# Turning the keys inside the scores' matmuls, and the last output product in quarters

## The chip, the cores and the metric

The kernel runs on one core of a Trainium2 chip. The metric is device time in microseconds. Three runs of the kernel before took 295.28, 295.98 and 296.2 us; the median is 295.98. The engines are TensorE (PE in the profile; PEld is its loading of stationary operands), VectorE (DVE), ScalarE (ACT), GpSimd (POOL) and SyncE (SP, which here only issues transfers).

## The reference

Two stages follow each other. The first is a gated linear attention, a recurrence over 768 positions for 4 batches of 8 heads of 48 dimensions:

```python
for t in range(S):
    state = alpha[:, :, t, :, None] * state + np.einsum('bhd,bhe->bhde', k[:, :, t], v[:, :, t])
    y[:, :, t] = np.einsum('bhd,bhde->bhe', q[:, :, t], state)
```

The heads' outputs side by side are x, 384 wide. The second stage is a gated state-space layer: `proj = x @ w_in` (384 by 1024) gives a value and a gate half of 512; `h = a * h + val` runs along the positions; the result is `(silu(gate) * h) @ w_out` (512 by 384).

## The kernel before, in words

Of the two versions in the file, `general` is a fallback that a test of the inputs selects; only `fast` runs here. It cuts the 4 x 768 positions into N = 12 groups m of 256, three to a batch, and each group into two chunks c of 128.

**Attention by chunks.** VectorE makes running products of alpha with a scan (`prod`, L664) and the inverse products with a second (`inv`, L685). Queries are multiplied by the products, keys by their inverses (Z, L694). With that scaling the recurrence becomes an ordinary masked matrix product within a chunk plus a state carried between chunks. Z has position along the free axis and head dimension along partitions. The eight heads form four pairs p, with the two heads i of a pair on partitions 0 to 47 and 64 to 111. The steps for one chunk are these.

- `keys` (L707, L708): for the state, the scaled keys must have position on partitions. Four TensorE transposes (one per pair, against the identity matrix) write them to a PSUM bank, and ScalarE copies that bank to `ktm`. The last chunk of a batch needs no state, so it has no such step: 20 of 24 chunks have it.
- `scores` (L717): eight products of 48 rows, keys stationary and queries moving, 128 by 128 each. The two heads of a pair go to two different banks. Each fp32 product is two instructions.
- `masks`: the near head's scores are multiplied by a triangular mask on VectorE straight from PSUM (L734); the far head's are copied by ScalarE (L729) and masked by GpSimd (L730).
- `state` (L766, L769), `values` (L745), `carried` (L756): the chunk's update of the state, the product of masked scores with v, and the contribution of the state before the chunk. The last two add up in PSUM tiles `ys`.
- `join` copies ys to SBUF and moves rows by transfer into `xT`, the input of the second stage.

**Second stage.** `block(n, cc)` makes one quarter cc of the 512 inner columns: twelve instructions of 256 columns on TensorE (L801: six for the value, six for the gate), the scan `hh` on VectorE (L809), Silu on ScalarE (L816), and their product f on GpSimd (L817). `output(n)` multiplies f by w_out: sixteen instructions of 384 columns (L831), of which the last quarter's come last. ScalarE copies the two results of 128 by 384 out (L839), in the last pass VectorE does (L841), and SP stores them (L842).

**Order.** The order of the program is written by hand; the engines run their own instructions in that order and meet through semaphores. The first groups are handled separately before the loop. Pass n of the loop then handles, interleaved, the second stage of group n, the attention of group m = n + 1, and on VectorE the products of group n + 2. Those products are a generator, `products(n + 2)`, whose steps `go` puts between the other work: first the transpose of alpha (L650) and small steps, then the prod scan, then the inv scan, then the transpose of k, its product with the inverses, the transpose of q and its product. In pass 1, group m = 2 comes from inputs in natural layout, so the passes' bodies differ.

In a pass n > 1 TensorE's order is: keys of both chunks, scores of both chunks, blocks 0 and 1, state/values/state/carried, blocks 2 and 3, output. In pass n = 1 it is: blocks 0 and 1, keys, scores, block 2, state/values/carried, block 3, output. `products`' first step stands ahead of the masks, so VectorE transposes alpha while the scores run.

**PSUM.** There are eight banks: one for the state `st`; b0, b1 and b6, through which `mm` rotates for blocks, key transposes and outputs; and the four banks b23 (a pair of banks in one tile), b4 and b5, which `pair_of` gives out in turn to scores and to ys.

Of the kernel before, what the change touches and what calls it, by code (L numbers as in the profile page):

```python
# [10 lines left out]
FP32 = mybir.dt.float32  # L11
# [335 lines left out]
def fast(  # L347
# [33 lines left out]
    def pool(name, bufs, **kw):  # L381
        return ctx.enter_context(tc.tile_pool(name=name, bufs=bufs, **kw))
# [1 line left out]
    const = pool("const", 1)  # L384
    p1 = pool("p1", 1)
    p2 = pool("p2", 2)
    p3 = pool("p3", 3)
    p4 = pool("p4", 4)


    ps_st = pool("ps_st", 1, space=PS)
    ps = pool("ps", 1, space=PS)
    next_mm, next_pair = itertools.cycle("016"), itertools.cycle((0, 1))

    def mm(*dims, b=None):
        return ps.tile([C, *dims], FP32, tag=f"b{b or next(next_mm)}", name="mm")

    def pair_of(*dims, dtype=FP32):
        if next(next_pair):
            return [ps.tile([C, *dims], dtype, tag=f"b{b}", name="pair") for b in (4, 5)]  # L400
        t = both()
        n = dims[0] * dims[1]
        return [t[:, i, 0:n].rearrange("p (x y) -> p x y", x=dims[0]).bitcast(dtype) for i in range(2)]

    def both():
        return ps.tile([C, 2, 4 * C], FP32, tag="b23", name="pair")


    NR = 2
# [60 lines left out]
    mask = const.tile([C, C], FP32, name="mask")  # L470
    a_log = const.tile([NI, C], FP32, name="a_log")
    a_dec = const.tile([C, NI], FP32, name="a_dec")
    ktms = [const.tile([C, 4, 2, 64], FP32, name=f"ktm{i}") for i in range(2)]


    aT = const.tile([C, 4 * GC + 1], FP32, name="aT")
# [20 lines left out]
    def constants():  # L497
        nc.vector.memset(first, FLOOR)
        make_identity(nc, ident)
        for name in "akq":  # L500
            nc.vector.memset(natural(name, 0)[:, :, :, D:64], 1.0)

        nc.gpsimd.memset(mask, 1.0)
        nc.gpsimd.affine_select(out=mask, in_=mask, compare_op=ALU.is_ge, fill=0.0, base=0,
                                channel_multiplier=-1, pattern=[[1, C]])
        for t in vs:
            nc.gpsimd.memset(t[:, :, :, D:64], 0.0)
        for name in "akq":
            nc.gpsimd.memset(natural(name, 1)[:, :, :, D:64], 1.0)
        for t, x in ((minus, -1.0), (start_p, FIRST_PRODUCT), (last, 0.0), (aT[:, 4 * GC:], 0.0), (one, 1.0)):  # L510
            nc.vector.memset(t, x)
        for m in range(2):
            for name in "akq":
                nc.gpsimd.memset(raw_bufs[m][name].rearrange("p h n -> p (h n)")[:, G * H * 64:], 1.0)
# [72 lines left out]
        nc.vector.tensor_copy(out=flag, in_=fl)  # L587


    Zs = {}  # L590

    def turned(name, m, c, tp):

# [2 lines left out]

    def natural_qk(m, name, c, tp):

        if m not in Zs:
            Zs[m] = p2.tile([C, 4, 2, GC], FP32, tag="Z", name="Z")  # L600
        turned(name, m, c, tp)

        def times():
            i, by = {"k": (1, invs), "q": (0, prods)}[name]
            cols = ds(c * C, C)
            if m < 1:
                by = (inv_c[c][:, 1:] if name == "k" else prod_c[c]).rearrange("p (h n) -> p h n", h=4)
            else:
                by = by[:, :, cols]
            nc.vector.tensor_mul(Zs[m][:, :, i, cols], tp, by)  # L610
        return times

    def check_alpha(m):
# [32 lines left out]
    def products(m, al=None):  # L646
# [40 lines left out]
        yield  # L687
        if m < NAT:
            return
        Z = Zs[m] = p2.tile([C, 4, 2, GC], FP32, tag="Z", name="Z")  # L690
        for name, i, by in (("k", 1, invs), ("q", 0, prods)):
            turn(name, Z[:, :, i])
            yield
            nc.vector.tensor_mul(Z[:, :, i], Z[:, :, i], by)  # L694
            yield


# [3 lines left out]
    def keys(m, c, b=None):  # L701

        if (m % NG) * G + c == NG * G - 1:
            return
        tp = mm(4, C, b=b)
        for p in range(4):
            nc.tensor.transpose(tp[:, p, :], Zs[m][:, p, 1, ds(c * C, C)], ident)  # L707
        nc.scalar.activation(ktms[c].rearrange("p a i d -> p a (i d)"), tp, AF.Copy)  # L708

    def scores(m, c):  # L710
        Z = Zs[m]
        cols = ds(c * C, C)
        sc = pair_of(4, C)
        for p in range(4):
            for i in range(2):
                rows = ds(64 * i, D)
                nc.tensor.matmul(sc[i][:, p, :], Z[rows, p, 1, cols], Z[rows, p, 0, cols], start=True, stop=True)  # L717
        As[m, c] = p2.tile([C, 2, 4, C], FP32, tag="A", name="A"), sc

    def masks(m, c):  # L720
        masks_far(m, c)
        masks_near(m, c)

    def mask_all():
        return mask[:, None, :].to_broadcast([C, 4, C])

    def masks_far(m, c):
        A, sc = As[m, c]
        nc.scalar.activation(A[:, 1], sc[1], AF.Copy)  # L729
        nc.gpsimd.tensor_mul(A[:, 1], A[:, 1], mask_all())  # L730

    def masks_near(m, c):
        A, sc = As[m, c]
        nc.vector.tensor_mul(A[:, 0], sc[0], mask_all())  # L734

    def values(m, c):
        v_sb = vs[m % NV]
        A, _ = As.pop((m, c))
        if c == 0:
            ys[m] = pair_of(2, GC) if m else [mm(2, GC, b=b) for b in "06"]  # L740
        for i in range(2):
            for e in range(2):
                for s in range(2):
                    p = 2 * s + e
                    nc.tensor.matmul(ys[m][i][ds(64 * s, 64), e, ds(c * C, C)], v_sb[:, c, 2 * p + i, :],  # L745
                                     A[:, i, p, :], start=(c == 0 and e == 0), stop=False, skip_group_check=True)

    def carried(m, c):
        ch = (m % NG) * G + c
        if not ch:  # L750
            return
        for e in range(2):
            for s in range(2):
                for i in range(2):
                    p, rows = 2 * s + e, ds(64 * i, D)
                    nc.tensor.matmul(ys[m][i][ds(64 * s, D), e, ds(c * C, C)], S_sbs[ch - 1][rows, p, :],  # L756
                                     Zs[m][rows, p, 0, ds(c * C, C)], start=False, stop=True,
                                     skip_group_check=True)

    def state(m, c):  # L760
        ch = (m % NG) * G + c
        if ch == NG * G - 1:
            return
        for p in range(4):
            for i in range(2):
                nc.tensor.matmul(st[ds(64 * i, 64), p, :], ktms[c][:, p, i, :], vs[m % NV][:, c, 2 * p + i, 0:D],  # L766
                                 start=(ch == 0 and p == 0), stop=(ch == NG * G - 2), skip_group_check=True)
        S_sbs[ch] = p2.tile([C, 4, D], FP32, tag="S_sb", name="S_sb")
        nc.scalar.activation(S_sbs[ch], st, AF.Copy)  # L769
# [53 lines left out]

    def output(n):
        b, g = divmod(n, NG)
        os = [mm(DM) for c in range(G)]

        def part(ccs):
            for c in range(G):
                for cc in ccs:  # L830
                    nc.tensor.matmul(os[c], fs[n][:, cc, ds(c * C, C)], w_out[:, cc, :],  # L831
                                     start=(cc == 0), stop=(cc == NI - 1))

        def finish():
            part(range(split, NI))
            for c in range(G):
                o_sb = p3.tile([C, DM], FP32, tag="o_sb", name="o_sb")
                if n < N - 1:
                    nc.scalar.activation(o_sb, os[c], AF.Copy)  # L839
                else:  # L840
                    nc.vector.tensor_copy(out=o_sb, in_=os[c])  # L841
                nc.sync.dma_start(out=out[b, ds(g * GC + c * C, C), :], in_=o_sb)  # L842

        split = NI - 1 if n else NI // 2
        part(range(split))
        return finish


# [66 lines left out]
    next(steps)  # L915
    masks_near(0, 1)

    k10, q10 = (ps.tile([C, 4, C], FP32, tag=f"b{b}", name="pair") for b in (4, 5))
    natural_qk(1, "q", 0, q10)
    q_sb = p1.tile([C, 4, C], FP32, tag="q_sb", name="q_sb")  # L920
    nc.scalar.activation(q_sb, q10, AF.Copy)
    nc.gpsimd.tensor_mul(Zs[1][:, :, 0, 0:C], q_sb, prods[:, :, 0:C])
    check_alpha(1)
    values(0, 1)
    state(0, 1)
# [61 lines left out]
    for n in range(1, N):  # L987
# [25 lines left out]
            loads(n + 3)  # L1013
        if n + 2 < N:
            load_v(n + 2, SP)
        if att:
            for c in range(G):
                keys(m, c)
            for c in range(G):
                scores(m, c)  # L1020
        go(1)
        if att:
            for c in range(G):
                masks(m, c)
        if n > 1:
            block(n, 0)
            if n == N - 1:
                next(end, None)
            go(1)
            block(n, 1)  # L1030
            go(1)
            attend()
            go(2)
            block(n, 2)
        else:
            block(n, 2)
            go(1)
            attend()
            go(1)
        go(1)  # L1040
        block(n, 3)
        go(10)
# [48 lines left out]
```

## Time and profile before

| | before |
|---|---|
| median of three runs | 295.98 us |
| the profiled execution | 295.81 us |
| its span | 294.1 us |
| TensorE busy | 280.9 us, 96% of the span |
| VectorE busy | 224.9 us, 76% |
| GpSimd busy | 113.7 us, 39% |
| ScalarE busy | 99.5 us, 34% |

The profile is of one execution. Its span is from the first to the last recorded instruction; 1.7 us of its time lie around that. A row of the groups gives the line, engine, operation, tile written and tiles read, shape and count, then busy time and mean duration in ns. Matmuls are pipelined and overlap, so their durations add to more than the time they take, and the distance from one start to the next says more. In the timeline, a row is a run of equal instructions: start in us, length in us, engine, line, operation, tile, shape and count. A last bracket tells how long the engine stood idle before the row and what it waited for.

### The profile page before, as it was taken

What the parts mean: (1) busy time and instruction counts of PE and PEld (TensorE: products, weight loads), DVE (VectorE), ACT (ScalarE), POOL (GpSimd) and SP (SyncE); (2) the same over time, 40 slices, a digit from 0 to 9 for tenths busy, and PEclk for the clock granted to TensorE, in tenths of its full rate; (3) what the DMA queues carried; (4) which work ended last, traced back from release to release, by engine and by line L of the source; (5) the groups of instructions that cost most, each with busy time, mean ns of one, the idle gap of its engine ahead of it and who ended that gap; (6) DMA issues with size and microseconds to landing.
All of it is one profiled execution on the core that took longest, in us unless ns stands there. A gap on an engine that the chain in (4) does not pass through costs nothing.

```text
span 294.1 us, 6126 instructions
## 1 busy us (share of the span) xinstructions
PE 280.9 (96%) x2345; PEld 226.1 (77%) x2345; DVE 224.9 (76%) x269; ACT 99.5 (34%) x220; POOL 113.7 (39%) x116
## 2 busy tenths in 40 slices
PE   7679999999999999999999999999999999999991
PEld 6468877886886896886886896886886886886870
DVE  5898896999996799798699699699699695312311
ACT  2447634433432432432432431431431531331110
POOL 7136792275612612642613513542513523401110
PEclk9999999999999999999999999999999999999999
DMA  9999979999991991991991792991891401101101
GB/s 130 163 175 285 356 128 168 234 271 217 264 177 54 237 167 33 244 187 39 246 171 31 199 213 48 228 196 33 226 204 29 111 10 33 54 15 28 54 7 61
DMA packets 71231, 42.09 MB, mean 143 GB/s; under 512 B 47492, under 2 KB 70536, under 8 KB 71192
## 3 DMA queue, kind: packets, MB, share of 16 engines
q1 hardware_dynamic: 69760, 40.96, 68.5%
q0 software_dynamic: 384, 0.44, 0.7%
q8 instruction: 20, 0.33, 0.5%
q10 hardware_dynamic: 1048, 0.20, 0.4%
q14 instruction: 19, 0.16, 0.2%
HBM read 33.33 MB, written 4.72 MB: 129 GB/s over the span
## 4 chain that ended last, share of the span: by engine, by line
PE 91%; DVE 6%; ACT 1%; issue 0%; DVEq 0%; ACTq 0%
PE mm L801 44%; PE mm L831 21%; PE pair L717 8%; PE pair L745 7%; PE pair L756 3%; PE st L766 3%; PE mm L707 2%; PE st L880 1%; DVE Z L610 1%; PE pair L595 1%; DVE inv L642 1%; DVE prod L664 1%; DVE inv L681 1%; DVE A L734 0%; DVE prod L632 0%
## 5 line engine op out<-in xcount | busy, mean ns | idle before, releaser
L801 PE MATMUL mm<-xT,w_in 128*128 128x256 f32 x576 | 131.1, 384 | 0.0
L801 PEld LDWEIGHTS mm<-xT,w_in 128*128 128x128 f32 x576 | 107.3, 190 | 18.1 <-issue 2.0
L817 POOL TENSOR_TENSOR f<-sg,hh 128x256 f32<-128x256 f32 x48 | 59.0, 1230 | 96.3 <-DVE hh L809 48.6
L831 PE MATMUL mm<-w_out,f 128*128 128x384 f32 x192 | 64.4, 487 | 0.0
L730 POOL TENSOR_TENSOR A<-A,mask 128x512 f32<-128x512 f32 x24 | 30.0, 1271 | 66.6 <-ACT A L729 66.6
L831 PEld LDWEIGHTS mm<-w_out,f 128*128 128x128 f32 x192 | 36.2, 190 | 23.1 <-POOL w_out L555 0.6
L816 ACT ACTIVATE sg<-mm 128x256 f32<-128x256 f32 x48 | 18.4, 384 | 93.9 <-PE mm L801 91.8
L809 DVE TENSOR_TENSOR_SCAN hh<-a_dec,hh,mm 128x256 f32<-128x256 f32 x32 | 23.2, 726 | 20.2 <-PE mm L801 20.1
L734 DVE TENSOR_TENSOR A<-pair,mask 128x512 f32<-128x512 f32 x24 | 16.1, 688 | 27.5 <-ACT A L729 17.7
L664 DVE TENSOR_TENSOR_SCAN prod<-aT,first 128x1024 f32<-128x1024 f32 x10 | 28.1, 2811 | 0.1
L717 PE MATMUL pair<-Z 48*128 48x128 f32 x384 | 25.1, 279 | 1.2 <-DVE first L660 0.9
L685 DVE TENSOR_TENSOR_SCAN inv<-aT,last 128x1025 f32<-128x1025 f32 x10 | 26.0, 2596 | 0.3
L717 PEld LDWEIGHTS pair<-Z 48*128 48x128 f32 x384 | 22.6, 187 | 3.5 <-issue 2.1
L839 ACT ACTIVATE o_sb<-mm 128x384 f32<-128x384 f32 x22 | 10.8, 491 | 42.8 <-PE mm L831 42.8
L745 PE MATMUL pair<-A,v 128*64 128x128 f32 x352 | 21.3, 274 | 0.0
L745 PEld LDWEIGHTS pair<-A,v 128*64 128x64 f32 x352 | 19.1, 137 | 0.0
L650 DVE STREAM_TRANSPOSE aT<-raw_a 128x1024 f32<-128x1024 f32 x9 | 18.4, 2041 | 0.0
L650 DVE STREAM_TRANSPOSE Z<-raw_q 128x1024 f32<-128x1024 f32 x9 | 18.2, 2020 | 0.0
L650 DVE STREAM_TRANSPOSE Z<-raw_k 128x1024 f32<-128x1024 f32 x9 | 18.1, 2015 | 0.0
L729 ACT ACTIVATE A<-pair 128x512 f32<-128x512 f32 x24 | 13.3, 598 | 7.0 <-PE pair L717 5.7
L766 PEld LDWEIGHTS st<-v,ktm 128*64 128x64 f32 x320 | 11.4, 137 | 3.9 <-issue 3.0
L769 ACT ACTIVATE S_sb<-st 128x192 f32<-128x192 f32 x20 | 6.6, 331 | 19.8 <-PE st L766 11.1
(119 smaller groups left out, 255.3 us busy)
## 6 DMA issues: line engine op xcount, KB each, us to landing
raw_k<-in_k_dram SPq DMA_DIRECT2D x24, 192.0 KB, 5.4
raw_q<-in_q_dram SPq DMA_DIRECT2D x24, 192.0 KB, 6.2
v<-in_v_dram SPq DMA_DIRECT2D x24, 192.0 KB, 6.4
out_dram<-o_sb SPq DMA_DIRECT2D x24, 192.0 KB, 1.9
raw_a<-in_alpha_dram SPq DMA_DIRECT2D x23, 192.0 KB, 4.0
raw_a<-in_alpha_dram SPq DMA_DIRECT2D x18, 176.0 KB, 4.2
raw_k<-in_k_dram SPq DMA_DIRECT2D x18, 176.0 KB, 5.7
raw_q<-in_q_dram SPq DMA_DIRECT2D x18, 176.0 KB, 6.6
```

The source lines that it names most:

```text
L650: nc.vector.transpose(out=to.rearrange("p h (c j) -> p h j c", j=NT), in_=raw_bufs[m % NR][name].rearrange("p h (j d) -> p h j d", d=D)[:, ...
L664: nc.vector.tensor_tensor_scan(out=prod, data0=al, data1=first.rearrange("p h n -> p (h n)"), initial=0.0, op0=ALU.mult, op1=ALU.max)
L685: nc.vector.tensor_tensor_scan(out=inv[:, ::-1], data0=aT[:, ::-1], data1=lasts[:, 0:4 * GC + 1][:, ::-1], initial=0.0, op0=ALU.mult, op1= ...
L717: nc.tensor.matmul(sc[i][:, p, :], Z[rows, p, 1, cols], Z[rows, p, 0, cols], start=True, stop=True)
L730: nc.gpsimd.tensor_mul(A[:, 1], A[:, 1], mask_all())
L745: nc.tensor.matmul(ys[m][i][ds(64 * s, 64), e, ds(c * C, C)], v_sb[:, c, 2 * p + i, :], A[:, i, p, :], start=(c == 0 and e == 0), stop=Fal ...
L766: nc.tensor.matmul(st[ds(64 * i, 64), p, :], ktms[c][:, p, i, :], vs[m % NV][:, c, 2 * p + i, 0:D], start=(ch == 0 and p == 0), stop=(ch = ...
L801: nc.tensor.matmul(pj, w_in[cc][:, kk, vg, :], xT[:, kk, :], start=(kk == 0), stop=(kk == NK - 1))
L809: nc.vector.tensor_tensor_scan(out=hh, data0=a_dec[:, cc:cc + 1].to_broadcast([C, GC]), data1=pv, initial=prev_h[cc][:, GC - 1:GC] if n % ...
L816: nc.scalar.activation(sg, pg, AF.Silu)
L817: return lambda: nc.gpsimd.tensor_mul(fs[n][:, cc, :], sg, hhs.pop((n, cc)))
L831: nc.tensor.matmul(os[c], fs[n][:, cc, ds(c * C, C)], w_out[:, cc, :], start=(cc == 0), stop=(cc == NI - 1))
```

## The change

Four things change.

- The transposes of the keys in groups m = 2 to 11 are gone as instructions. The tile of the scaled queries gets 48 more columns on each side that hold an identity matrix on the rows of each head. GpSimd writes them once at the start with eight copies. The scores' product of a chunk that needs turned keys runs over 176 columns, 128 of queries and 48 of identity; so the 48 extra output columns are that head's keys with position on partitions. ScalarE copies them to `ktm` by two instructions, one for each head of the pairs. Chunks without a state step run over 128 columns as before.
- 176 columns for four pairs fill more than a bank per head, so a chunk's scores take four banks: two tiles `four0` and `four1` of two banks each. They are the four banks of b23, b4 and b5, given over to a new pool in pass 1. Scores of chunk 0, scores of chunk 1, and ys each take all four, one after the other.
- Therefore the order changes. In a pass n > 1 TensorE's is now: scores of chunk 0, block 0, scores of chunk 1, block 1, state/values/state/carried, blocks 2 and 3, output. In pass 1 it is: blocks 0 and 1, scores of chunk 0, block 2, scores of chunk 1, state/values/carried, block 3, output. Masks come straight after their scores. The steps of `products` move back: the alpha transpose comes after block 0 (in pass 1 after the first masks), the prod scan after block 1 (in pass 1 after the second masks), the inv scan after the values.
- In the last pass the output product is made in four pieces of 128 by 192, the second in the bank of `st`. Each is copied out and stored by itself.

Z is split into the tiles `Zk` and `Zq`, of which there are two each as there were two of Z. The core of the diff:

```diff
-    ktms = [const.tile([C, 4, 2, 64], FP32, name=f"ktm{i}") for i in range(2)]
+    ktms = [const.tile([C, 2, 4, 64], FP32, name=f"ktm{i}") for i in range(2)]
+    Zks = [const.tile([C, 4, GC], FP32, name=f"Zk{i}") for i in range(2)]
+    Zqs = [const.tile([C, 4, GC + 2 * D], FP32, name=f"Zq{i}") for i in range(2)]
+
+    def Z_of(m, i):
+        return Zks[m % 2] if i else Zqs[m % 2][:, :, D:D + GC]
...
+        for t in Zqs:
+            for i in range(2):
+                rows = ds(64 * i, D)
+                for at in (0, D + GC):
+                    nc.gpsimd.tensor_copy(out=t[rows, :, at:at + D], in_=ident[rows, None, rows].to_broadcast([D, 4, D]))
...
+    def scores_keys(m, c):
+
+        whole = (m % NG) * G + c < NG * G - 1
+        sc = fours()
+        n = C + D
+        of_c = ds(c * n, n) if whole else ds(D + c * C, C)
+        for p in range(4):
+            for i in range(2):
+                rows = ds(64 * i, D)
+                to = sc[i][:, p // 2, ds(p % 2 * n + (0 if whole or c else D), n if whole else C)]
+                nc.tensor.matmul(to, Z_of(m, 1)[rows, p, ds(c * C, C)], Zqs[m % 2][rows, p, of_c], start=True, stop=True)
+        halves = [t[:, :, 0:2 * n].rearrange("q b (p n) -> q b p n", p=2) for t in sc]
+        at = 0 if c else D
+        As[m, c] = p2.tile([C, 2, 4, C], FP32, tag="A", name="A"), [t[:, :, :, at:at + C] for t in halves]
+        masks_far(m, c)
+        masks_near(m, c)
+        if whole:
+            at = C if c else 0
+            for i in (1, 0):
+                nc.scalar.activation(ktms[c][:, i, :, 0:D].rearrange("q (b p) d -> q b p d", p=2),
+                                     halves[i][:, :, :, at:at + D], AF.Copy)
+
+    def fours():
+        return [ps_four.tile([C, 2, 4 * C], FP32, tag=f"four{i}", name="four") for i in range(2)]
...
+        if n < N - 1:
+            pieces = [(c, ds(0, DM), mm(DM)) for c in range(G)]
+        else:
+            halves = ds(0, DM // 2), ds(DM // 2, DM // 2)
+            places = [mm(DM // 2), st.rearrange("q p d -> q (p d)"), mm(DM // 2), mm(DM // 2)]
+            pieces = [(c, x, places.pop(0)) for c in range(G) for x in halves]
...
-        if att:
-            for c in range(G):
-                keys(m, c)
-            for c in range(G):
-                scores(m, c)
-        go(1)
-        if att:
-            for c in range(G):
-                masks(m, c)
-        if n > 1:
+        if n == 1:
+            at_first.close()
+            ps_four = pool("ps_four", 1, space=PS)
+            scores_keys(m, 0)
+            go(1)
+            block(n, 2)
+            scores_keys(m, 1)
+            go(1)
+            attend()
+            go(1)
+        else:
+            if att:
+                scores_keys(m, 0)
             block(n, 0)
             if n == N - 1:
                 next(end, None)
             go(1)
+            if att:
+                scores_keys(m, 1)
             block(n, 1)
             go(1)
             attend()
-            go(2)
+            go(1)
             block(n, 2)
-        else:
-            block(n, 2)
-            go(1)
-            attend()
-            go(1)
         go(1)
         block(n, 3)
         go(10)
```

## The prediction

> **What bounds the kernel now.** I read the page's busy times first, then the chain that ended last, then the groups, then TensorE's and VectorE's timelines around the first changed pass, because the change reorders exactly that.
>
> ```profile
> PE 280.9 (96%) x2345; PEld 226.1 (77%) x2345; DVE 224.9 (76%) x269; ACT 99.5 (34%) x220; POOL 113.7 (39%) x116
> ...
> PE 91%; DVE 6%; ACT 1%; issue 0%; DVEq 0%; ACTq 0%
> ...
> L717 PE MATMUL pair<-Z 48*128 48x128 f32 x384 | 25.1, 279 | 1.2 <-DVE first L660 0.9
> ```
>
> TensorE is busy 96% and carries 91% of the last chain. A matmul's time in this kernel is therefore time at the end, and so is every wait that TensorE gains. Durations of single matmuls overlap; the useful measure is from start to start. TensorE's timeline, pass n=1 and the start of n=2 (start, us, line, tile, count):
>
> ```profile
> 52.74 2.75 PE L801 MATMUL mm<-xT,w_in 128*128 128x256 f32 x12
> 55.33 0.60 PE L707 MATMUL mm<-ident,Z 128*128 128x128 f32 x4
> 55.86 2.06 PE L717 MATMUL pair<-Z 48*128 48x128 f32 x32
> 57.84 2.86 PE L801 MATMUL mm<-xT,w_in 128*128 128x256 f32 x12
> 60.63 0.67 PE L766 MATMUL st<-v,ktm 128*64 128x48 f32 x16
> 61.13 1.93 PE L745 MATMUL pair<-A,v 128*64 128x128 f32 x32
> 62.99 1.09 PE L756 MATMUL pair<-Z,S_sb 48*48 48x128 f32 x32
> 64.02 2.86 PE L801 MATMUL mm<-xT,w_in 128*128 128x256 f32 x12
> 66.71 5.32 PE L831 MATMUL mm<-w_out,f 128*128 128x384 f32 x16
> 71.87 1.04 PE L707 MATMUL mm<-ident,Z 128*128 128x128 f32 x8
> 72.84 2.06 PE L717 MATMUL pair<-Z 48*128 48x128 f32 x32
> ```
>
> No piece waits for another engine. The same twelve instructions of a projection block take 2.59 us between two full-array groups (52.74 to 55.33), 2.69 with a partial-array neighbour on one side (64.02 to 66.71) and 2.79 with one on both (57.84 to 60.63). Each crossing costs the block 0.10. The other side pays as well: single starts in the trace are 109 ns apart for key transposes, then 203 to the first scores; pairs of scores are 111.5 ns apart, but 0.10 more after the first. So one visit to the scores' tiling and back costs 0.09 + 0.10 + 0.10 + 0.10 = 0.39 us beyond its matmuls. Full-array starts are 216 ns apart at 256 columns and 322.5 at 384: 0.833 ns a column plus 2.5.
>
> VectorE's and GpSimd's timelines in the same pass:
>
> ```profile
> 55.81 2.04 DVE L650 STREAM_TRANSPOSE aT<-raw_a 128x1024 f32<-128x1024 f32 x1
> 58.28 1.29 DVE L734 TENSOR_TENSOR A<-pair,mask 128x512 f32<-128x512 f32 x2
> 60.14 2.76 DVE L664 TENSOR_TENSOR_SCAN prod<-aT,first 128x1024 f32<-128x1024 f32 x1
> 61.26 2.16 POOL L817 TENSOR_TENSOR f<-sg,hh 128x256 f32<-128x256 f32 x1 [0.51 <-ACT sg L816]
> 71.41 1.23 DVE L694 TENSOR_TENSOR Z<-Z,prod 128x1024 f32<-128x1024 f32 x1
> ```
>
> VectorE delivers Z of m=3 at 72.64; its scores start at 72.84. That is 0.2 us of reserve, held only because the eight key transposes stand in front. GpSimd's f product takes 2.16 us beside the 60.14 scan, 0.73 elsewhere.
>
> [...]
>
> **The change, part by part.** It touches m=2 to 11: six passes with two key chunks (m=3, 4, 6, 7, 9, 10), four with one (2, 5, 8, 11).
>
> 1. Key transposes go: 109 ns each, 8 per two-key pass (-0.872), 4 per one-key pass (-0.436).
> 2. 48 columns more per scores matmul: 128 columns take 106.7 + 2 x 2.5 = 111.5 ns a pair, 176 then 146.7 + 4.9 = 151.6, +40. A chunk is 16 matmuls, two for each fp32 product, so 8 pairs: +0.32. Bounds: 0 if weight loads set the pair, which 109 ns for single transposes contradicts; +0.64 if the pair did not overlap. I take +0.32.
> 3. The scores split around a block: one more visit to their tiling per pass, +0.39. Bounds 0 and 0.5; seen at each such crossing, so 0.39.
>
> A two-key pass: -0.872 + 0.64 + 0.39 = +0.16; a one-key pass: -0.436 + 0.32 + 0.39 = +0.27. In all 6 x 0.16 + 4 x 0.27 = **+2.05 us**.
>
> 4. Pass n=1, where little stands between the second scores and their use. Scores (2,0) start at 55.42; their eighth pair starts at 55.42 + 0.25 + 6 x 0.152 = 56.58; masks follow 0.42 later (0.38 before, plus 0.04 of stream), at 57.0. VectorE now does this near mask before the aT transpose, which moves from 55.81 to 57.61 (mask 0.61), then small steps, hh at 60.08, second near mask. That needs scores (2,1): block 56.83 to 59.62, eighth pair 60.50, mask 60.88 to 61.57; the scan follows at 61.49, not 60.14. Values need the four banks free: 61.65 instead of 61.2. ScalarE's second far copy ends at 61.48, but GpSimd first multiplies f (60.9 to 61.63). [...] the far mask runs 63.95 to 65.2. The last quarter of values, due at 62.94, waits for it: 65.25. Then 0.5 + carried 1.02 + block 2.70 + output 5.16 end at 74.65. VectorE meanwhile: scan end 63.95, 0.6 of small steps, inverse scan held by the far mask to 65.2, end 67.5, transpose, hh, product, transpose, product (1.87 + 0.60 + 1.11 + 2.06 + 1.23) = 74.3. Scores of m=3 start at 74.75, where TensorE alone would be at 71.87 + 0.27 + 0.09 = 72.23: **+2.5**. [...] I take 2.5 because the scan is queued before the mask.
>
> 5. Later passes, from the start S of the first scores: near mask S+1.6, hh S+3.1, aT transpose to S+5.8, second scores S+4.2 to 5.5, near mask S+6.1, hh S+7.3, scan S+7.9, inverse S+11.2, hh S+13.9, transpose k, hh, product k, transpose q, product q done S+21.6. TensorE returns at S+22.8 (two keys) or S+22.0 (one key; Z then S+21.2). Cover 0.8 us or more: nothing. The two checks (0.93 each) follow Z, before the next near mask at S+24.3. The far mask (S+6.75) precedes the scan (S+7.9), so no clash. Four-bank waits: second scores S+4.2 against key copies done S+3.2; values S+8.9 against S+7.2. Without this cover each would cost its excess, once a pass.
>
> 6. Key copies: 128x512 at 0.55 becomes two of 128x192, priced by S_sb's 0.33; ScalarE is 34% busy. Eight GpSimd identity copies of 48x192 at start, between the 128x512 memset's 0.53 and the 128x256 product's 0.73 each: 4 to 6 us, with six memsets (2.8) behind them. GpSimd's set-up then ends at 10 to 12 us instead of 6.0; its first far mask is at 12.87, so 0, at most 0.3 without that cover. No transfers change queue. Joins leave by S+12.3 and are due at S+24.2, 8.9 us needed at present.
>
> 7. Tail. Its copies are:
>
> ```profile
> 287.17 1.26 DVE L841 COPY o_sb<-mm 128x384 f32<-128x384 f32 x2 [4.99 <-PE mm L831]
> 287.76 1.03 SPq L842 DMA_DIRECT2D out_dram<-o_sb  x2
> ```
>
> Quarters: 32 matmuls of 162.5 ns, +0.04; the last copy falls from 0.56 to about 0.36. But four issues must pass SP, 0.33 each plus about 0.05 between: the last leaves about when it did. The landing is half as large. -0.3 to +0.4, I take -0.1. A 0.13 us hold in pass n=2's blocks (a 244 ns start and a crossing) disappears.
>
> Sum: 2.05 + 2.5 - 0.1 - 0.13 = +4.3. The profiled execution spans 294.1 and took 295.81; 1.7 lies around it. Span after 298.4, execution 300.1. The median of before, 295.98, is 0.17 above its profiled run; I predict **300.2**.
>
> **Rivals.** (a) The extra visit costs nothing[...]. Then 2.05 - 10 x 0.39 = -1.85, and with n=1 the total is +0.4: 296.4, no measurable change. It decides below 0.05 us per visit (4.3 - 10 x 0.34 = 0.9). Against it: every such crossing in the trace pays, with satisfied waits and without any. (b) VectorE becomes the bound: it has 20 us of work in a 22 us pass and waits for scores twice instead of once. If scans or masks come 1.3 us later than I list, each of eight passes lengthens by 0.4: 303.4. For it: 0.2 us reserve now; against: 0.8 us after. (c) n=1 is absorbed almost wholly[...]: 297.8. (d) [...]
>
> **Numbers.** My case [...]: 0.72, own range 299.0 to 301.5. (b) 0.13, (c) 0.07, (a) 0.06, (d) 0.02. Low end 297.6 takes in (c), high 303.4 takes in most of (b). A measurement tells about 0.3%, 0.9 us, from no change: (a) alone can end there or, with (c), below. Faster 0.04, same 0.04, slower 0.92.
>
> **What would show it.** Right: 128x176 pairs 152 ns apart; a block between two scores groups 2.79 us; two-key passes 22.77 instead of 22.61, one-key 22.0 instead of 21.72; values of n=1 waiting for GpSimd, m=3 scores near 74.75; no TensorE wait later. Wrong: blocks at 2.59 beside scores, (a); scores waiting for Zq each pass, (b); pairs far from 152 ns.

## The result and the profile after

The changed kernel takes **299.24 us** (median of 4 runs, 298.87 to 299.48), beside 295.96 for the kernel before (4 runs, 295.28 to 296.2): the ratio is 1.0114, 95% interval 1.0093 to 1.0134, clear of no change. The profiled execution took 299.08 us and spans 297.3, so 1.8 lies around it.

The page of the changed kernel, busy times, last chain and four groups (mean ns of one, then idle time before them):

```profile
PE 282.4 (95%) x2297; PEld 224.5 (76%) x2297; DVE 224.8 (76%) x271; ACT 100.3 (34%) x236; POOL 101.7 (34%) x124
...
PE 87%; DVE 5%; DMA 2%; POOL 1%; SPq 1%; issue 1%; ACT 1%; DVEq 0%; POOLq 0%; ACTq 0%
...
L862 POOL TENSOR_TENSOR f<-sg,hh 128x256 f32<-128x256 f32 x48 | 42.2, 879 | 106.7 <-ACT sg L861 85.2
...
L740 PE MATMUL four<-Zq,Zk 48*128 48x176 f32 (+1 forms) x320 | 28.1, 315 | 0.0
...
L675 DVE TENSOR_TENSOR_SCAN prod<-aT,first 128x1024 f32<-128x1024 f32 x10 | 22.8, 2278 | 0.1
...
L790 PE MATMUL four<-A,v 128*64 128x128 f32 x320 | 19.6, 274 | 2.0 <-POOL A L765 1.7
```

TensorE issues 48 matmuls fewer, yet is busy 1.5 us longer. Its scores wait for nothing (0.0); its values wait 1.7 us for GpSimd's mask. GpSimd, on the other hand, is busy 12 us less than before.

Two timelines carry the rest. First, a two-key pass, TensorE's timeline of the changed kernel, pass n=3 (start, us, line, tile, count):

```profile
96.49 1.46 PE L740 MATMUL four<-Zq,Zk 48*128 48x176 f32 x16
97.89 2.86 PE L846 MATMUL mm<-xT,w_in 128*128 128x256 f32 x12
100.67 1.46 PE L740 MATMUL four<-Zq,Zk 48*128 48x176 f32 x16
102.07 2.86 PE L846 MATMUL mm<-xT,w_in 128*128 128x256 f32 x12
104.86 0.67 PE L811 MATMUL st<-v,ktm 128*64 128x48 f32 x16
```

Both blocks lie between partial-array groups (`48*128` and `128*64` in the rows, where a block has `128*128`), and from start to start they take 2.78 and 2.79 us (100.67 - 97.89, 104.86 - 102.07). In the kernel before, blocks 0 and 1 of such a pass stood together, each with one such neighbour. No piece waits. Inside the scores the single starts alternate 7 and 142 ns: a pair of 176 columns takes 149.3 ns, where a pair of 128 took 111.5.

Second, pass n=1 with the start of the next, TensorE:

```profile
55.20 1.46 PE L740 MATMUL four<-Zq,Zk 48*128 48x176 f32 x16
56.59 2.86 PE L846 MATMUL mm<-xT,w_in 128*128 128x256 f32 x12
59.38 1.16 PE L740 MATMUL four<-Zq,Zk 48*128 48x128 f32 x16
60.47 0.67 PE L811 MATMUL st<-v,ktm 128*64 128x48 f32 x16
61.39 1.53 PE L790 MATMUL four<-A,v 128*64 128x128 f32 x24 [0.24 <-DVE A L765]
64.64 0.66 PE L790 MATMUL four<-A,v 128*64 128x128 f32 x8 [1.72 <-POOL A L765]
65.22 1.09 PE L801 MATMUL four<-Zq,S_sb 48*48 48x128 f32 x32
66.25 2.86 PE L846 MATMUL mm<-xT,w_in 128*128 128x256 f32 x12
68.94 5.32 PE L881 MATMUL mm<-w_out,f 128*128 128x384 f32 x16
74.19 1.46 PE L740 MATMUL four<-Zq,Zk 48*128 48x176 f32 x16
```

and VectorE with GpSimd in the same stretch:

```profile
57.36 2.06 DVE L661 STREAM_TRANSPOSE aT<-raw_a 128x1024 f32<-128x1024 f32 x1
...
60.54 0.73 POOL L862 TENSOR_TENSOR f<-sg,hh 128x256 f32<-128x256 f32 x1 [1.80 <-DVE hh L854]
60.64 0.69 DVE L765 TENSOR_TENSOR A<-four,mask 128x512 f32<-128x512 f32 x1 [0.24 <-PE four L740]
...
61.25 2.28 DVE L675 TENSOR_TENSOR_SCAN prod<-aT,first 128x1024 f32<-128x1024 f32 x1
61.29 3.30 POOL L765 TENSOR_TENSOR A<-A,mask 128x512 f32<-128x512 f32 x1
...
64.73 2.29 DVE L696 TENSOR_TENSOR_SCAN inv<-aT,last 128x1025 f32<-128x1025 f32 x1
...
72.57 1.22 DVE L705 TENSOR_TENSOR Zq<-Zq,prod 128x1024 f32<-128x1024 f32 x1
```

The far mask of (2,1) starts 0.04 us after the scan and takes 3.30 us, where the one before it took 1.29. It ends at 64.59, and the last quarter of the values starts at 64.64. Together with the 0.24 us for VectorE's mask before it, that is all the waiting which the change put into the passes. The scores of m=3 then start at 74.19. They do not wait: the output before them starts at 68.94, and 5.25 us from an output's start to the next scores is what pass n=3 has too (91.24 to 96.49).

At the end, VectorE's copies and SP's transfers:

```profile
290.26 0.36 DVE L892 COPY o_sb<-mm 128x192 f32<-128x192 f32 x1 [4.70 <-PE mm L881]
...
290.59 0.36 DVE L892 COPY o_sb<-st 128x192 f32<-128x192 f32 x1
290.65 1.78 SPq L893 DMA_DIRECT2D out_dram<-o_sb  x4
290.97 0.68 DVE L892 COPY o_sb<-mm 128x192 f32<-128x192 f32 x2
```

A copy takes 0.36 us, where a half took 0.56 before; but four transfers pass SP, and the last is issued 6.20 us after the output's start, not 6.01. From its issue to its landing it takes 3.49 us, not 3.67, and from there to the end 1.77, not 1.95. From output start to end it is 11.46 us, not 11.63.

Where the time went, from the start of one output product to the start of the next (us):

| stretch | before | after | difference |
|---|---|---|---|
| to the first output | 42.02 | 41.79 | -0.23 |
| pass n=1 (one key chunk) | 24.695 | 27.150 | +2.455 |
| n=3, 6, 9 (two keys) | 22.609 | 22.737 | +0.128 each |
| n=4, 7, 10 (one key) | 21.722 | 21.983 | +0.261 each |
| n=2, 5, 8 (two keys) | 22.305 | 22.300 | -0.005 each |
| n=11 | 15.837 | 15.837 | 0 |
| last output to the end | 11.63 | 11.46 | -0.17 |

The sum is +3.2, which is the difference of the spans (297.3 - 294.1). The first and the last row are no larger than what executions differ by: over the nine profiled executions of this study, the first output starts between 41.73 and 42.09, and the last stretch takes 11.17 to 11.77 us in the three that store halves and 11.46 to 11.80 in the six that store quarters. The passes alone lost 3.6 us.

Passes 2, 5 and 8 lose 0.13 us less by the change than 3, 6 and 9, which have the same work. In the kernel before, one start in block 3 of each of them came late (a 244 ns interval and then 320, in place of two of 216): block 3's gate half takes the PSUM bank from which VectorE's `hh` of block 2 reads, and in pass n=2 that `hh` ended only at 87.56, the late start being at 87.62. In the changed kernel all three delays are gone.

### The profile page after: what moved, and what is told of

Read it like the earlier page. It is cut to its first block, busy times and chain, and to the rows that moved or that the text cites. A ratio compares the mean times of both kernels' runs of the same rounds, so it can differ in the third digit from the quotient of the medians.

```text
span 297.3 us, 6040 instructions
## 1 busy us (share of the span) xinstructions
PE 282.4 (95%) x2297; PEld 224.5 (76%) x2297; DVE 224.8 (76%) x271; ACT 100.3 (34%) x236; POOL 101.7 (34%) x124
## 2 busy tenths in 40 slices
DMA packets 71519, 42.09 MB, mean 142 GB/s; under 512 B 47524, under 2 KB 70824, under 8 KB 71480
## 4 chain that ended last, share of the span: by engine, by line
PE 87%; DVE 5%; DMA 2%; POOL 1%; SPq 1%; issue 1%; ACT 1%; DVEq 0%; POOLq 0%; ACTq 0%
PE mm L846 43%; PE mm L881 21%; PE four L740 9%; PE four L790 6%; PE st L811 3%; PE four L801 3%; DMA raw_q<-in_q_dram 2%; SPq L438 1%; PE pair L727 1%; POOL A L765 1%; PE pair L608 1%; DVE prod L675 1%; DVE inv L692 1%; DVE aT L661 1%; PE pair L790 1%
## 5 line engine op out<-in xcount | busy, mean ns | idle before, releaser
L862 POOL TENSOR_TENSOR f<-sg,hh 128x256 f32<-128x256 f32 x48 | 42.2, 879 | 106.7 <-ACT sg L861 85.2
L881 PE MATMUL mm<-w_out,f 128*128 128x384 f32 (+1 forms) x200 | 63.4, 468 | 0.0
L740 PEld LDWEIGHTS four<-Zq,Zk 48*128 48x128 f32 x320 | 23.0, 186 | 8.6 <-PE mm L881 4.4
L740 PE MATMUL four<-Zq,Zk 48*128 48x176 f32 (+1 forms) x320 | 28.1, 315 | 0.0
L765 DVE TENSOR_TENSOR A<-four,mask 128x512 f32<-128x512 f32 x20 | 13.8, 692 | 17.5 <-PE four L740 17.5
L675 DVE TENSOR_TENSOR_SCAN prod<-aT,first 128x1024 f32<-128x1024 f32 x10 | 22.8, 2278 | 0.1
L790 PE MATMUL four<-A,v 128*64 128x128 f32 x320 | 19.6, 274 | 2.0 <-POOL A L765 1.7
L790 PEld LDWEIGHTS four<-A,v 128*64 128x64 f32 x320 | 17.3, 137 | 2.3 <-POOL A L765 2.0
L661 DVE STREAM_TRANSPOSE Zq<-raw_q 128x1024 f32<-128x1024 f32 x9 | 18.3, 2038 | 0.0
L661 DVE STREAM_TRANSPOSE Zk<-raw_k 128x1024 f32<-128x1024 f32 x9 | 18.2, 2025 | 0.0
L770 ACT ACTIVATE A<-four 128x512 f32<-128x512 f32 x20 | 11.9, 595 | 10.9 <-PE four L740 10.9
```

What stands on the lines that cost most here:

```text
L661: nc.vector.transpose(out=to.rearrange("p h (c j) -> p h j c", j=NT), in_=raw_bufs[m % NR][name].rearrange("p h (j d) -> p h j d", d=D)[:, ...
L675: nc.vector.tensor_tensor_scan(out=prod, data0=al, data1=first.rearrange("p h n -> p (h n)"), initial=0.0, op0=ALU.mult, op1=ALU.max)
L740: nc.tensor.matmul(to, Z_of(m, 1)[rows, p, ds(c * C, C)], Zqs[m % 2][rows, p, of_c], start=True, stop=True)
L765: engine.tensor_mul(to, src, by)
L862: return lambda: nc.gpsimd.tensor_mul(fs[n][:, cc, :], sg, hhs.pop((n, cc)))
L881: nc.tensor.matmul(o, fs[n][:, cc, ds(c * C, C)], w_out[:, cc, x], start=(cc == 0), stop=(cc == NI - 1))
```

## The experiments

Ratios are to runs of the kernel before on the same chip: for the split alone, no extra columns, the first pass as it was and the far mask on VectorE their median is 296.17 us (18 runs), for the other three 296.13 (35 runs). One execution of each kernel was profiled. Passes are measured as in the table.

### The split alone

The kernel before, keys still transposed, four separate halves of scores, but the second chunk's scores and masks moved behind block 0 in the passes 2 to 10:

```diff
-            for c in range(G):
+            for c in range(G if n == 1 else 1):
                 scores(m, c)
 ...
-            for c in range(G):
+            for c in range(G if n == 1 else 1):
                 masks(m, c)
 ...
             block(n, 0)
 ...
+            if att:
+                scores(m, 1)
+                masks(m, 1)
             go(1)
             block(n, 1)
```

> The kernel before with one edit: in passes 2 to 10 the second chunk's scores and masks stand after block 0 instead of beside the first chunk's. No instruction is added or removed. My theory [...]: 9 passes x 0.39 = +3.5 us against before, all of it on TensorE's starts, blocks beside scores at 2.79 us; about 299.5 us. Rival (a visit is free, the loss comes from what the columns and waits cost): 0, 296.0 us. A rival in which VectorE's later masks do the harm: a loss too, but with TensorE waiting for another engine in these passes.

Measured: 308.71 us (306.94 to 309.77, 4 runs), ratio 1.0431 (1.0391 to 1.0471). The theory's 299.5 missed by 9 us; of the possibilities named, the third, TensorE waiting for VectorE, came on top of the visit's price. That price is there: block 1 of pass n=2, between scores and state, takes 2.79, the second scores 1.09. But about 8.2 us of waits and restarts came with it. TensorE's waits in the passes (total us, times, longest; short holds are not in them), one of them from its timeline, and VectorE's work before it:

```profile
PE mm L801 <- DVE hh L809: 6.3, 6, 1.4
```

```profile
89.44 1.56 PE L801 MATMUL mm<-xT,w_in 128*128 128x256 f32 x6 [1.44 <-DVE hh L809]
...
85.45 2.01 DVE L650 STREAM_TRANSPOSE Z<-raw_k 128x1024 f32<-128x1024 f32 x1
87.50 1.23 DVE L694 TENSOR_TENSOR Z<-Z,inv 128x1024 f32<-128x1024 f32 x1
88.64 0.74 DVE L809 TENSOR_TENSOR_SCAN hh<-a_dec,hh,mm 128x256 f32<-128x256 f32 x1
```

Pass n=2 shows how: 24.411 us against 22.305 is 0.395 for the visit and, for the most part, one interval between block 3's matmuls of 1.82 us where 0.216 is due. After each of the six waits the next interval is 320 ns in place of 216, the same as in the changed kernel's trace after the first matmul of a block that follows scores: each restart took another 0.10 from TensorE here. VectorE's scan for block 2 ran only at 88.64, behind the transpose of k and its product, because the order of the kernel before puts the first five steps of the products ahead of block 2, and VectorE reaches them later now: it stands idle for 2.35 us before the second mask, since the scores and ScalarE's copy of them come later. The changed kernel puts three there: the steps begin one place later, and `go(2)` becomes `go(1)`. So the move of the steps is no bookkeeping: by the next run, which has both parts of it, the split without it costs nearly four times as much. Which part does how much was not separated.

### The split with its order of steps

As above, with the changed kernel's order in the passes 2 to 10; keys still transposed, 128 columns, pass 1 untouched:

```diff
-            for c in range(G):
-                scores(m, c)
-        go(1)
-        if att:
-            for c in range(G):
-                masks(m, c)
+            scores(m, 0)
         if n > 1:
+            if att:
+                masks(m, 0)
             block(n, 0)
 ...
             go(1)
+            if att:
+                scores(m, 1)
+                masks(m, 1)
             block(n, 1)
             go(1)
             attend()
-            go(2)
+            go(1)
             block(n, 2)
```

> The kernel before with the changed kernel's whole order in passes 2 to 10: scores split around block 0, masks straight after, steps of the products one place later. Key transposes, 128 columns and pass 1 as before. The run with the split alone lost 12 us because VectorE's hh of block 2 stood behind the k transpose and its product; here it stands before both. My theory: 9 visits x 0.395 = +3.55, less 3 x 0.13 for a hold of block 3 in passes 2, 5, 8 that this order removes: +3.15 us against before, passes of 22.565, 23.00 and 22.12 us, no wait of TensorE in them. Rival (a visit is free): passes of 22.17, 22.61, 21.72, total -0.4. Rival (VectorE is the bound in this order): waits of TensorE for VectorE again, over +5.

Measured: 299.37 us (299.27 to 299.86, 4 runs), ratio 1.0118 (1.0091 to 1.0146). The theory's 3.15 us came out as 3.2. The passes take 22.569, 23.004 and 22.118 us for n=2, 3 and 4, and no TensorE wait is left in them. Pass n=2 of this kernel:

```profile
76.79 1.16 PE L717 MATMUL pair<-Z 48*128 48x128 f32 x16
77.88 2.86 PE L801 MATMUL mm<-xT,w_in 128*128 128x256 f32 x12
80.67 0.67 PE L766 MATMUL st<-v,ktm 128*64 128x48 f32 x16
```

Passes 3 and 4 are 0.395 and 0.396 longer than before; pass 2 is 0.264 longer, 0.395 less its lost delay of 0.13. The same holds for 5 to 10 within 0.002. The extra visit to the scores' tiling therefore costs 0.395 us, by itself, in every pass, with nothing waiting.

### No extra columns

The changed kernel with all scores at 128 columns; the keys' copies that would read the missing columns are left out too:

```diff
         sc = fours()
+        whole = False
 ...
-        if whole:
-            at = C if c else 0
-            for i in (1, 0):
-                nc.scalar.activation(ktms[c][:, i, :, 0:D]..., halves[i][:, :, :, at:at + D], AF.Copy)
```

> The changed kernel with all scores 128 columns wide and without the copies of the turned keys; the state of groups 2 to 11 is then made from old keys, so the output is another one. The split and pass 1 stay. My theory (48 more columns cost 38 ns a pair of matmuls): 16 chunks x 8 pairs x 0.038 = -4.8 us against the changed kernel, about 294.4. Rival (columns hide under the weight loads): 0, 299.2. Rival (VectorE is nearly the bound): less than 4.8, with scores waiting for Zq.

Measured: 295.68 us (294.64 to 296.88, 14 runs), ratio 0.9976 (0.9954 to 0.9999). The passes are 21.695, 22.132 and 21.681 us for n=2, 3 and 4: against the changed kernel 0.605 less with two key chunks, 0.302 with one. That is eight pairs of 37.8 ns for each chunk, the difference of the pair intervals (149.3 - 111.5). A two-key pass closes from the other side as well: 22.609 - 0.872 for eight transposes + 0.395 for the visit = 22.132, as measured for n=3.

The median is 1.3 us above the expected 294.4, and the profiled execution, 296.20, is 1.8 above it. Of the latter, 1.65 us has nothing to do with columns. TensorE's clock in the 40 slices of this kernel's span, and the block behind the waiting values of pass n=1:

```profile
PEclk9999999997999999999999999999999999999997
```

```profile
66.17 4.51 PE L842 MATMUL mm<-xT,w_in 128*128 128x256 f32 x12
```

The tenth slice (66 to 74 us) shows a lower clock, and this block takes 4.34 us to the next group instead of 2.69: six of its starts are 427 ns apart, not 216. Pass n=1 is 1.34 us longer here than in the changed kernel's profiled execution, which waits as long in the same place and shows no such block. How many of the other 13 executions had such a block, and so how much of the median's 1.3 it explains, is open.

### The first pass as it was

The changed kernel, with pass n=1 in its old form (transposed keys, halves of scores side by side, masks before block 2):

```diff
 ...
         if n == 1:
-            at_first.close()
-            ps_four = pool("ps_four", 1, space=PS)
-            scores_keys(m, 0)
+            keys(m, 0)
+            for c in range(G):
+                scores(m, c)
             go(1)
+            for c in range(G):
+                masks(m, c)
             block(n, 2)
-            scores_keys(m, 1)
             go(1)
             attend()
 ...
+            if n == 2:
+                at_first.close()
+                ps_four = pool("ps_four", 1, space=PS)
```

> The changed kernel with pass 1 as before (key transposes, both scores together, masks after the first step of the products); the four banks are given over at pass 2. My theory: the 2.45 us that pass 1 gained go, but VectorE's Z of m=3 is now needed with no key transposes in front, so about 0.7 of them come back as a wait of the m=3 scores for VectorE: -1.7 us against the changed kernel, about 297.5. Rival (pass 1's wait is hidden later by slack): 0, 299.2.

Measured: 298.89 us (298.22 to 299.42, 5 runs), ratio 1.0085 (1.0058 to 1.0112). That is 1.4 above the theory and not clearly less than the changed kernel (1.0093 to 1.0134). Pass n=1 is back at 24.688 us, 2.46 less; but the stretch after it takes 24.552 where the changed kernel's takes 22.300. From this kernel's timeline, VectorE and TensorE:

```profile
56.75 2.05 DVE L661 STREAM_TRANSPOSE aT<-raw_a 128x1024 f32<-128x1024 f32 x1 [1.14 <-DMA raw_a<-in_alpha_dram]
...
69.52 3.49 PE L881 MATMUL mm<-w_out,f 128*128 128x384 f32 x10 [0.99 <-DVE hh L854]
73.93 1.46 PE L740 MATMUL four<-Zq,Zk 48*128 48x176 f32 x16 [0.92 <-DVE Zq L705]
```

From start to start the two waits are 1.15 and 1.09 us, together the 2.25. The output waits for VectorE's last `hh`, the scores of m=3 for VectorE's Z. Two causes meet. VectorE began its transpose 1.14 us late, for a load that SP had issued late, behind a slow issue of v (3.49 us, 2.28 in the kernel before). And the eight transposes of keys (0.97 with their crossing) that stood ahead of the scores of m=3 are gone, so that TensorE is back for Z sooner: in the kernel before, Z was done at 72.64, when TensorE without these transposes would have been there since 71.96 (71.87 + 0.09 for the crossing). From Z's end to the first scores it takes 0.15 us here, so an estimate for the second cause alone is 0.83 (72.64 + 0.15 - 71.96).

The late load is no property of this kernel. In the profiled execution of the quarters alone (below), whose pass n=1 is that of the kernel before with all its transposes, the same transpose waited 0.76 us for the same load, the output 0.64 for `hh`, and the stretch after pass n=1 took 23.197 us instead of 22.305. So what is shown is that in this execution nearly all of the 2.46 us turned into waits for VectorE. How much of the gain stays without a late load was not measured; by the estimate it is 1.6 (2.46 - 0.83).

### The far mask on VectorE

The changed kernel, with the one far mask that meets the scan done by VectorE from PSUM, so that GpSimd has none to do there:

```diff
     def masks_far(m, c):
         A, sc = As[m, c]
+        if (m, c) == (2, 1):
+            half_mask(nc.vector, m, c, 1, sc[1])
+            return
```

> The changed kernel with one mask moved: the far mask of group 2's second chunk, the one that GpSimd ran beside the scan, is done by VectorE straight from PSUM; ScalarE's copy for it goes too. My theory: TensorE's wait of 2.0 us in values disappears, but VectorE has 0.6 us more and ends Z of m=3 no earlier, so the wait moves to the m=3 scores (near 1.7 us there): -0.3 us against the changed kernel, 298.9. Rival (the far mask alone is the loss of pass 1): -2.0, 297.2.

Measured: 298.77 us (298.49 to 298.85, 4 runs), ratio 1.0080 (1.0054 to 1.0107). Pass n=1 takes 25.933 us, 1.22 less than in the changed kernel; the stretch after it 23.010, 0.71 more. VectorE and TensorE in this kernel's timeline:

```profile
62.11 2.28 DVE L675 TENSOR_TENSOR_SCAN prod<-aT,first 128x1024 f32<-128x1024 f32 x1
...
62.34 1.97 PE L793 MATMUL four<-A,v 128*64 128x128 f32 x32 [0.97 <-DVE A L765]
...
72.54 1.23 DVE L705 TENSOR_TENSOR Zq<-Zq,prod 128x1024 f32<-128x1024 f32 x1
...
73.91 1.46 PE L740 MATMUL four<-Zq,Zk 48*128 48x176 f32 x16 [0.64 <-ACT o_sb L893]
```

The values' wait falls from two pieces (0.24 and 1.72) to one of 0.97, now for VectorE's two masks. TensorE is then back before Z: its output starts at 67.95, the scores would be due 5.25 later at 73.20, and start at 73.91, 0.14 after Zq ends. (The row names ScalarE's copy of the output, whose end is near; the same copy holds nothing up in the changed kernel.) So GpSimd's mask beside the scan is what held pass n=1, as the theory had it, and over half of what its removal gives (0.71 of 1.22) is lost to the next wait. The waits were expected elsewhere, though: none at the values and near 1.7 us at the scores, for 0.97 and 0.64 found; the net, -0.5 on the spans of the two passes, is near the -0.3 expected.

### Quarters

The kernel before with the last output product in quarters (with a fourth buffer for the output's copies, as in the changed kernel); and the same with `go(1)` for `go(2)` ahead of block 2:

```diff
-            go(2)
+            go(1)
             block(n, 2)
```

> The kernel before with the last output product in quarters and nothing else. From the changed kernel's trace: the stretch from the start of that product to the end 11.63 to 11.46, so -0.17 us, 295.8; rival: the two more issues of SP cost what the shorter copies save, 0.

> The same with one step of the products moved: one step instead of two between the values and block 2, so that hh of block 2 stands before the product of k. Theory: the 0.13 us hold in passes 2, 5 and 8 goes: -0.4 more, -0.55 against before, 295.4. Rival: the later transpose of q makes the scores wait for Z, +0.3 or more a pass.

Quarters alone: 295.78 us (295.51 to 298.07, 14 runs), ratio 0.9999 (0.9982 to 1.0016). From output start to end it took 11.55 us, 0.08 less than before; this can't be told from nothing. With the moved step: 295.40 us (295.1 to 296.98, 22 runs), ratio 0.9981 (0.9968 to 0.9994). Blocks 2 and 3 of pass n=2, first in the kernel before, then in this one:

```profile
83.60 5.58 PE L801 MATMUL mm<-xT,w_in 128*128 128x256 f32 x24
```

```profile
83.52 5.45 PE L801 MATMUL mm<-xT,w_in 128*128 128x256 f32 x24
```

The moved step gave -0.38, for -0.4 expected. Passes 2, 5 and 8 take 22.172 us, 0.13 less, and the others are as before: the step is what made the late starts. This is the fastest kernel of the study, by about 0.2% against the kernel before, with an interval that ends just below no change.

## Why the prediction was right, and which terms were off

299.24 us lies 1.0 below the 300.2 predicted, inside the likeliest case's own range of 299.0 to 301.5. The mechanism was the forecast one, and about 0.3 of the 1.0 is chance: the first and the last stretch, which differ as much between executions. The sum, term by term, on spans:

| term | predicted | measured |
|---|---|---|
| steps 1 to 3 in the passes 2 to 10 | 6 x 0.16 + 3 x 0.27 = +1.77 | 6 x 0.128 + 3 x 0.261 = +1.55 |
| pass n=1, its own steps 1 to 3 included | +2.78 (output's start 66.71 to 69.49) | +2.455 |
| late starts that vanish | -0.13 (one pass) | -0.39 (three) |
| last output to the end | -0.1 | -0.17 |
| before the first output | 0 | -0.23 |
| sum | +4.3 | +3.2 |

**Steps 1 and 3 held.** The transposes were worth 109 ns each; the passes of the kernel without extra columns come out with that price to the nanosecond (22.609 - 0.872 + 0.395 = 22.132). The visit was put at 0.39 us and measured 0.395 for in and out, alone, by the split with its order of steps. The changed kernel's trace has the parts of a visit as longer starts: 247 ns in place of 142 after the first pair of scores, 320 in place of 216 after the first matmul of the block. What TensorE does in that time is not shown. Rival (a), a free visit, is refuted: with it the split with its order of steps would have gained 0.4 us, and it lost 3.2.

**Step 2 was mis-sized.** A pair grew by 37.8 ns, not 40: over the 15 chunks of those passes -0.27. The step added two fixed costs of 2.5 ns to 146.7 for the wide pair; the trace has 149.3, as if only one counted there.

**Step 4 named the right mechanism, 0.33 too long.** Beside the scan the far mask takes 3.30 us instead of 1.29 and ends late, the values wait 1.72 for it, and nothing later recovers it. The forecast let the far mask begin only when a scan of 2.46 us had ended, and take 1.25. In the trace the scan took 2.28, and the mask ended 1.06 after it: 64.59, and with the 0.23 by which this run was ahead, 64.82 beside the forecast 65.2. Both orders of the two stand in the traces. In the cases that follow, the one that began first took its usual time, and the other longer. Here the scan led by 0.04 us, took 2.28, and the mask 3.30 where another took 1.29; the same happened in four passes of the split alone (in pass n=3 the scan at 102.71 took 2.28, the mask at 102.75 took 3.31). In pass n=1 of the kernel before the mask began first (59.49, the scan at 60.14), took 1.26, and the scan 2.76 where 2.28 is the changed kernel's mean. What holds the later one is not shown. A lead of 0.04 us (the same in the run without extra columns) is little: that the scan would be first was forecast, from its place in the queue, but with no margin to speak of. The scores of m=3 start at 74.19, for 74.75 forecast: 0.23 of that is the run's lead, the rest the earlier end of the mask.

**Step 5 held.** In no pass from n=2 on does TensorE wait. There Z is done 1.26 to 1.33 us before its scores, for a forecast cover of 0.8 or more. The comparison with 0.2 us before was misread, though: that is the reserve of m=3 alone, and in the later passes of the kernel before Z is done 4.0 to 4.5 us ahead. The change used up most of that room. Rival (b), VectorE as the bound, is refuted for this kernel, and so is (d), the rival at 318 us, in which scan and far mask would meet in every pass: from n=2 on they hardly do. (In four passes of the split alone they did, and the values did not wait for it.) Rather the opposite: over all passes the first scan fell from 2811 ns to 2278 in the mean and GpSimd's product from 1230 (59.0 us for 48 in the profile before) to 879. In the kernel before, a GpSimd mask was running when each scan of passes 1 to 9 began; in the changed kernel, from n=2 on, the mask has ended by then or ends at most 0.16 us later, and one product of a pass meets a scan (1.57 to 1.68 us, 0.73 elsewhere). But rival (b) is not far: with the split but the old order of steps, TensorE lost 8.2 us to waits (the split alone). Rival (c) is refuted by the 2.455.

**Step 6 held.** GpSimd's eight copies took 0.33 us each, less than the 4 to 6 us in all that bounded them; its set-up ended at 8.7 us, ahead of its first mask at 12.7. The 0.23 before the first output lies within what executions differ by (41.73 to 42.09), with or without that set-up.

**Step 7's tail** came out at -0.17, -0.08 when tried alone: near the predicted -0.1, but executions with halves differ among themselves by 0.6 us there, so that no effect of the quarters is shown. Its other term failed by a count: the late start was seen in pass n=2 and credited once, though the same order recurs in passes 5 and 8.

What decides the sign is thus: merged keys save 0.27 us in a two-key pass (0.872 - 0.605) and 0.13 in a one-key pass (0.436 - 0.302), and the order that came with four banks for one chunk (4 x 176 = 704 columns a head, where the program's tiles have 512 in a bank) adds a visit of 0.395. Each pass loses before any wait is counted. The other three quarters of the +3.2 are pass n=1, where the first use of the new order has no cover: 0.26 of its 2.455 are steps 1 to 3, nearly all of the rest its two waits (0.24 and 1.72).

## What to carry to other kernels

The work moved into a matmul was not free here, where 48 columns more took 37.8 ns a pair: price the columns that such a move adds, and the visit to another tiling (0.395 us here) that comes with its larger PSUM footprint, before counting what it removes. When a stall goes, look at once for what is late next: here, in the executions profiled, two ways of removing the wait in pass n=1 ended in a wait for Z. And where a kernel repeats passes in a period, count a delay in every pass of its kind, not in the one that was looked at.

## What the hardware showed that was not expected

In one kernel's profiled execution (no extra columns) TensorE ran at half its rate for part of the block that follows the 1.72 us wait in pass n=1: six starts are 427 ns apart for 256 columns, where 216 is usual, and the block took 4.34 us to the next group in place of 2.69, +1.65. The mean granted clock of that execution is 0.989, beside 0.998 in the changed kernel's. The changed kernel had the same wait of 1.72 us, and its block took 2.69 (66.25 to 68.94). What lowered the clock is not shown. If the wait did, which one case can't tell, this stall of under 2 us cost nearly twice its length in that execution.
